# Load order at the start of an S5 plus gated-FFN kernel: the second x tile moves to the common load queue, parameter rows move behind a mean, and the dummy matmuls are cut finer

## The chip, the cores and the metric

The kernel runs on one core of a Trainium2 chip. The metric is the time of one execution in microseconds, as the device measures it. The profile's own span (first to last instruction) is about 1.3 us shorter.

## The reference, cut to what matters

```python
xn = layernorm(x)                                   # x: 2048 x 512, bf16
A  = 2*Re(scan(Lam_bar, xn @ B_bar^T) @ C^T) + xn*Dskip   # Lam_bar = exp(exp(log_dt)*(Lambda_re + i*Lambda_im))
Bo = (gelu(xn @ w_gate) * (xn @ w_up)) @ w_down     # 512 -> 1376 -> 512
out = x + A + Bo
```

The kernel works in 4 blocks of 512 rows, of 4 tiles of 128 rows each. The three parameter vectors (`log_dt`, `Lambda_re`, `Lambda_im`, 1 KB each) are small, but the scan needs them transposed on chip.

## The kernel before

A small list scheduler written in Python orders ScalarE, VectorE and GpSimd statically; TensorE and the load queue (issued by SyncE, "SP") keep the order of the program text. The engines wait for each other by semaphores. In the start, tiles 0 and 1 are only centred (mean taken off), transposed on TensorE and multiplied with the first columns of the weights as these arrive; the division by the root of the variance follows later.

```python
# loads: x tile 0 on the load queue, x tile 1 on ScalarE's queue
ld_x0(0)
GATE["par"] = S.order_behind(ld_x0(1, "scalar", [wrm]), GATE["table"])
for k in range(KD):                       # KD = 4 pieces of 128 KB of each of two weights
    if k in (1, 3):
        ld_x0((k + 3) // 2)               # tiles 2 and 3
    ld_wk(WG, WGc, ins["B_w_gate"], k)
    ld_wk(WU, WUc, ins["B_w_up"], k)
ld_w(WG, WGc, ins["B_w_gate"], 1)
ld_w(WU, WUc, ins["B_w_up"], 1)

def load_par():                           # three rows, on ScalarE's queue, one behind the other
    for q, nm in enumerate(("A_log_dt", "A_Lambda_re", "A_Lambda_im")):
        GATE["par"] = S.order_behind(S.dma(... PROW.ap[4*q:4*q+4, :] ..., queue="scalar", after=[half]), GATE["par"])

def tr_par():                             # on the load queue; waits for all three rows
    S.dma(lambda e: e.dma_start_transpose(PAR.ap..., PROW16.ap), 4096, reads=PROWq, writes=[PAR], tag="tr_par", issue=900.0)
# ... cut ...
nwarm = 7                                 # wide dummy matmuls, so that TensorE's clock rises
PE(fwarm, ...)
def fill(n): ...                          # n narrow dummy matmuls, 128 x 128
# ... cut ...
load_par()
load_W()                                  # the last two weight pieces
tr_par()                                  # <- stands on the load queue AHEAD of all that follows there
S.order_behind(ACT(... X[1] -> NM1 ..., "mean1"), GATE["par"])    # the mean of tile 1, on ScalarE
# ... cut: centring, transposes, first matmuls; then, on the load queue in this order:
#   TR(0): 4 transposes of block 0's x;  ld_x(1): x of block 1;  load_B(): transposed B;  TR(1): block 1's x
```

Of the kernel before, what the change touches and what calls it, by code (L numbers as in the profile page):

```python
# [10 lines left out]
ACTF = mybir.ActivationFunctionType  # L11
# [331 lines left out]
L, D, P, F = 2048, 512, 512, 1376  # L343
# [12 lines left out]
def d_dve_ts4x(n): return 220.0 + 0.26 * n  # L356
D_TINY = 160.0
def d_act(n, ptr=0): return 190.0 + 0.833 * n + 90.0 * ptr
# [3 lines left out]
def build(nc, ins, out):  # L362
    with ExitStack() as es:
        E = es.enter_context
        S = Sched(nc, es)
# [6 lines left out]
        def ring(parent, name, n):  # L372
            return [A.sub(parent, "%s%d" % (name, i), i) for i in range(n)]
# [14 lines left out]
        X = ring(X_all, "X", NT)  # L388
# [73 lines left out]
        ACT = lambda fn, dur, r, w, tag="", after=(): S.op("scalar", fn, dur, r, w, tag, after)  # L462
# [3 lines left out]
        GATE = {"before_gelu": [], "nh": 0}  # L466
        SCR = A.alloc("SCR", [1], F32)
        half = V(lambda e: e.memset(HALF.ap, 0.5), D_TINY, [], [HALF], "half")
        wrm = S.order_behind(V(lambda e: e.memset(WRM.ap, 0.0), 150, [], [WRM], "wrm"), half)
# [5 lines left out]
        NM1, SUM0 = A.alloc("NM1", [1], F32), A.alloc("SUM0", [1], F32)  # L475
# [16 lines left out]
        def ld_x0(j, queue="sync", after=()):  # L492
            return S.dma(lambda e, j=j: e.dma_start(X[j].ap, x2[128 * j:128 * (j + 1), :]), 128 * 1024, writes=[X[j]], tag="ld_x0", queue=queue, after=after)
        ld_x0(0)
        GATE["par"] = S.order_behind(ld_x0(1, "scalar", [wrm]), GATE["table"])
        for k in range(KD):
            if k in (1, 3):
                ld_x0((k + 3) // 2)
# [5 lines left out]
        def load_par():  # L504
            for q, nm in enumerate(("A_log_dt", "A_Lambda_re", "A_Lambda_im")):
                GATE["par"] = S.order_behind(S.dma(lambda e, q=q, nm=nm: e.dma_start(PROW.ap[4 * q:4 * q + 4, :], ins[nm].rearrange("(s p) -> s p", p=128)),
                      1024, writes=[PROWq[q]], tag="ld_" + nm, queue="scalar", after=[half]), GATE["par"])

        def tr_par():
            S.dma(lambda e: e.dma_start_transpose(PAR.ap.rearrange("p q t -> p (q t)").unsqueeze(1), PROW16.ap), 4096,  # L510
                  reads=PROWq, writes=[PAR], tag="tr_par", issue=900.0)
# [12 lines left out]
        def load_W():  # L524
            ld_w(WG, WGc, ins["B_w_gate"], 2)
            ld_w(WU, WUc, ins["B_w_up"], 2)
# [146 lines left out]
        def cent_T(j, k0, k1, bank, eng="A", c0=0):  # L673
            pt = PS[bank].bitcast(BF16)[:, c0:c0 + 128 * (k1 - k0)]

            def f(e):
                ins_ = None
                for k in range(k0, k1):
                    ins_ = e.transpose(pt[:, 128 * (k - k0):128 * (k - k0 + 1)], XN[j].ap[:, 128 * k:128 * (k + 1)], IDN.ap)  # L679
                return ins_  # L680
            PE(f, 56.0 * (k1 - k0), [XNp[j][k0 > 0] if j < 2 else XN[j], IDN], [BANK[bank]], "T0")
            dst, src = XC_all.ap[:, k0:k1, 128 * j:128 * (j + 1)], pt.rearrange("p (q t) -> p q t", t=128)
            w = XCs[j] if k1 - k0 == KD else [XCs[j][k0 > 0]]
            sc = 1.0 if j else 1.0 / D
            if eng == "A":
                GATE["evTA"] = ACT(lambda e: e.activation(dst, src, ACTF.Copy, scale=sc), d_act(128 * (k1 - k0)), [BANK[bank]], w, "evT")
                return GATE["evTA"]
            return V(lambda e: e.tensor_scalar(dst, src, sc, None, ALU.mult), 110 + 0.6 * 128 * (k1 - k0), [BANK[bank]], w, "evT")
# [233 lines left out]
                for j in range(4):  # L922
                    seed(j); hidden(j); states(j); store(j)

        nwarm = 7
        ones, ones4 = nc.const_aps.tensor(1.0, (128, 128), BF16), nc.const_aps.tensor(1.0, (128, 512), BF16)
        wb = 4

# [6 lines left out]
        def fill(n):  # L935
            def f(e):
                ins_ = None
                for _ in range(n):
                    ins_ = e.matmul(PS[wb][:, 0:128], ones, ones, start=True, stop=True)  # L939
                return ins_  # L940
            PE(f, 56.0 * n, [], [BANK[wb]], "fill")
# [3 lines left out]
        def ch(*ops):  # L945
            for op in ops:
                tail_op[0] = S.order_behind(op, tail_op[0])
        def sub(j):
            return V(lambda e: e.tensor_scalar(XN[j].ap, X[j].ap, MVt[0][j].ap[:, 0:1], None, ALU.subtract),
                     d_dve_ts4x(512), [X[j], MVt[0][j]], [XN[j]], "sub")  # L950
        load_par()
        load_W()
        tr_par()
        S.order_behind(ACT(lambda e: e.activation(H0[3].ap[:, 0:D], X[1].ap, ACTF.Copy, scale=-1.0 / D, accum_out=NM1.ap), d_act(512) + 190,
                           [X[1]], [H0[3], NM1], "mean1"), GATE["par"])

        def cent(j, n):
            c0, c1 = (0, 128) if n == 0 else (128, D)
            if j == 0:
                f = lambda e: e.tensor_scalar(XN[j].ap[:, c0:c1], X[j].ap[:, c0:c1], float(D), SUM0.ap, ALU.mult, ALU.subtract)  # L960
            else:
                f = lambda e: e.tensor_scalar(XN[j].ap[:, c0:c1], X[j].ap[:, c0:c1], NM1.ap, None, ALU.add)
            return V(f, 100 + 0.5 * (c1 - c0), [X[j], NM1 if j else SUM0], [XNp[j][n]], "sub")

        ch(V(lambda e: e.tensor_reduce(SUM0.ap, X[0].ap, mybir.AxisListType.X, ALU.add), 600, [X[0]], [SUM0], "sum0"))
        ch(cent(0, 0), cent(0, 1))
        fill(1)
        ch(cent_T(0, 0, 1, 7, "V"))
        ch(cent(1, 0), cent(1, 1))
        fill(4)  # L970
        def ks(k, j, w_, first=False):
            for u in range(2):
                GT_k(k, j, u, w_, first)
# [7 lines left out]
        for j in range(2):  # L981
            ks(1, j, [0, 1])
        ch(*stats(0, 2)); ch(sub(2)); ch(*stats(0, 0)); ch(*stats(0, 1))
        op, mn0, qb0, rq0 = root(0, 0, 3)
        ch(op)
        ch(*stats(0, 3)); ch(sub(3))
        ch(recip(qb0, rq0))
        op, mn3, qb3, rq3 = root(0, 3, 4)
# [63 lines left out]
def bass_parallel_sum__ssm_conv_s5__geglu_ffn__prompt_kernel(  # L1052
    nc: bass.Bass,
    A_x: bass.AP,
    A_Lambda_re: bass.AP,
    A_Lambda_im: bass.AP,
    A_B_re: bass.AP,
    A_B_im: bass.AP,
    A_C_re: bass.AP,
    A_C_im: bass.AP,  # L1060
    A_log_dt: bass.AP,
    A_Dskip: bass.AP,
    B_x: bass.AP,
    B_w_gate: bass.AP,
    B_w_up: bass.AP,
    B_w_down: bass.AP,
    out: bass.AP,
):
    ins = {
        "A_x": A_x, "A_Lambda_re": A_Lambda_re, "A_Lambda_im": A_Lambda_im,  # L1070
        "A_B_re": A_B_re, "A_B_im": A_B_im, "A_C_re": A_C_re, "A_C_im": A_C_im,
        "A_log_dt": A_log_dt, "A_Dskip": A_Dskip,
        "B_w_gate": B_w_gate, "B_w_up": B_w_up, "B_w_down": B_w_down,
    }
    build(nc, ins, out)
# [28 lines left out]
```

## Time and profile before

| | median us | range | runs |
|---|---|---|---|
| before, first series | 177.41 | 177.30 to 177.45 | 6 |
| before, the four later series | 177.41, 177.24, 177.35, 177.31 | 176.95 to 178.19 | 11 each |
| profiled execution of before | 176.98 (span 175.66) | | 1 |

From the page: the span, and the chain that ended last as shares of the span.

```profile
span 175.7 us, 2494 instructions
...
PE 98%; issue 1%; DVE 0%
```

TensorE (PE) is the chain, almost alone. So the time is decided by when TensorE gets going, and by any wait that it meets later. The timeline of TensorE at the start (start us, duration us, engine, line, what, count, and in brackets the idle time before it):

```profile
3.95 0.51 PE L939 MATMUL PS<-const-bfloat16-1.0 128*128 128x128 bf16 x4
4.57 0.38 PE L700 MATMUL PS<-arena 128*128 128x256 bf16 x2
...
7.42 1.02 PE L700 MATMUL PS<-arena 128*128 128x512 bf16 x4
```

L939 are dummies; L700 are the first useful matmuls, at 4.57; the 128x512 ones at 7.42 belong to k=2 and wait for a weight piece that landed at 7.29. Later in the same timeline:

```profile
18.24 5.13 PE L842 MATMUL PS<-arena 128*128 128x512 bf16 x23
23.20 1.48 PE L816 MATMUL PS<-arena 128*128 128x192 bf16 x16
24.52 14.00 PE L748 MATMUL PS<-arena 128*128 128x512 bf16 x70
38.36 1.89 PE L842 MATMUL PS<-arena 128*128 128x512 bf16 x8
```

L842 at 18.24 needs the transposed x of block 0, L748 at 24.52 needs B. No brackets, so no idle time of note.

ScalarE's timeline ("ACTq" is its sequencer, which issues loads):

```profile
0.99 0.38 ACTq L493 DMA_DIRECT2D arena<-in_A_x_dram  x1
1.42 0.57 ACTq L506 DMA_DIRECT2D arena<-in_A_log_dt_dram  x1
2.02 0.26 ACTq L506 DMA_DIRECT2D arena<-in_A_Lambda_re_dram  x1
...
2.31 0.31 ACTq L506 DMA_DIRECT2D arena<-in_A_Lambda_im_dram  x1
...
5.04 1.42 ACT L686 ACTIVATE arena<-PS 128x128 bf16<-128x128 bf16 x3 [1.16 <-PE PS L679]
```

All three rows (L506) have left by 2.6 us, before ScalarE has anything to evict (L686, at 5.04). And the load queue's own timeline:

```profile
8.14 2.37 SPq L510 DMA_TRANSPOSE arena<-arena  x1
10.56 5.18 SPq L735 DMA_TRANSPOSE arena<-arena  x4
15.79 0.58 SPq L478 DMA_DIRECT2D arena<-in_A_x_dram  x1
16.41 3.06 SPq L521 DMA_TRANSPOSE arena<-in_A_B_re_dram  x1
```

L510 is the transpose of the parameters, issued at 8.14, as soon as the last weight piece is off; then the four transposes of block 0 (L735), x of block 1 (L478), B (L521).

### The profile page before, as it was taken

What the parts mean: (1) busy time and instruction counts of PE and PEld (TensorE: products, weight loads), DVE (VectorE), ACT (ScalarE), POOL (GpSimd) and SP (SyncE); (2) the same over time, 40 slices, a digit from 0 to 9 for tenths busy, and PEclk for the clock granted to TensorE, in tenths of its full rate; (3) what the DMA queues carried; (4) which work ended last, traced back from release to release, by engine and by line L of the source; (5) the groups of instructions that cost most, each with busy time, mean ns of one, the idle gap of its engine ahead of it and who ended that gap; (6) DMA issues with size and microseconds to landing.
All of it is one profiled execution on the core that took longest, in us unless ns stands there. A gap on an engine that the chain in (4) does not pass through costs nothing.

```text
span 175.7 us, 2494 instructions
## 1 busy us (share of the span) xinstructions
PE 172.1 (98%) x868; PEld 84.0 (48%) x883; DVE 159.8 (91%) x279; ACT 95.5 (54%) x185; POOL 10.7 (6%) x24
## 2 busy tenths in 40 slices
PE   8999999999999999999999999999999999999995
PEld 3545564644544444444644444444464444444454
DVE  6987999996999989889899999989999899999941
ACT  5476677899876898383576792000667970000000
POOL 3122030201000000002100000000000000000000
DMA  5899999695998000002015000002001000000311
GB/s 155 241 320 174 215 178 222 126 132 113 191 298 225 0 4 2 0 30 85 8 39 111 1 0 0 4 0 90 30 0 30 4 0 0 0 0 0 120 64 60
DMA packets 32420, 14.36 MB, mean 82 GB/s; under 512 B 23736, under 2 KB 32408, under 8 KB 32408
## 3 DMA queue, kind: packets, MB, share of 16 engines
q1 hardware_dynamic: 32240, 14.07, 35.5%
q8 instruction: 7, 0.11, 0.3%
q10 hardware_dynamic: 168, 0.13, 0.2%
q14 instruction: 5, 0.04, 0.1%
HBM read 6.46 MB, written 2.10 MB: 49 GB/s over the span
## 4 chain that ended last, share of the span: by engine, by line
PE 98%; issue 1%; DVE 0%
PE PS L883 37%; PE PS L842 32%; PE PS L748 16%; PE PS L711 4%; PE PS L700 3%; PE PS L816 3%; PE PS L932 2%; PE PS L679 1%; PE PS L939 0%; DVE arena L901 0%
## 5 line engine op out<-in xcount | busy, mean ns | idle before, releaser
L883 PE MATMUL PS<-arena 128*128 128x512 bf16 (+3 forms) x317 | 65.9, 366 | 0.3
L842 PE MATMUL PS<-arena 128*128 128x512 bf16 x257 | 57.1, 379 | 0.4
L883 PEld LDWEIGHTS PS<-arena 128*128 128x128 bf16 (+1 forms) x323 | 30.8, 98 | 35.2
L842 PEld LDWEIGHTS PS<-arena 128*128 128x128 bf16 x264 | 25.8, 98 | 30.2
L786 DVE TENSOR_TENSOR_SCAN arena<-arena 128x512 bf16<-128x512 f32 x32 | 38.9, 1255 | 0.0
L857 ACT ACTIVATE arena<-PS 128x512 bf16<-128x512 f32 x33 | 19.8, 599 | 25.8 <-DVE arena L901 16.7
L748 PE MATMUL PS<-arena 128*128 128x512 bf16 (+1 forms) x134 | 28.0, 366 | 0.1
L861 ACT ACTIVATE arena<-PS 128x512 bf16<-128x512 f32 x33 | 19.8, 600 | 5.1 <-PE PS L842 5.1
L875 ACT ACTIVATE PS<-arena 128x512 f32<-128x512 bf16 (+2 forms) x17 | 9.6, 581 | 19.7 <-DVE arena L901 19.0
L748 PEld LDWEIGHTS PS<-arena 128*128 128x128 bf16 x136 | 13.3, 98 | 14.1
L757 ACT ACTIVATE arena<-PS 128x512 bf16<-128x512 f32 x32 | 17.7, 592 | 2.1 <-PE PS L748 2.1
L901 DVE TENSOR_TENSOR arena<-PS,arena 128x512 bf16<-128x512 f32 (+2 forms) x17 | 10.9, 653 | 6.4 <-PE PS L883 6.4
L863 DVE TENSOR_TENSOR arena<-arena 128x512 bf16<-128x512 bf16 x33 | 13.1, 416 | 1.7 <-ACT arena L861 1.6
L775 DVE TENSOR_TENSOR arena<-arena 128x4096 bf16<-128x4096 bf16 (+1 forms) x5 | 9.2, 1859 | 0.8 <-ACT arena L606 0.8
L773 DVE TENSOR_TENSOR arena<-arena 128x4096 bf16<-128x4096 bf16 (+1 forms) x5 | 9.2, 1859 | 0.1
L798 DVE TENSOR_TENSOR arena<-arena 128x4096 bf16<-128x4096 bf16 x4 | 9.2, 2288 | 0.1
L799 DVE TENSOR_TENSOR arena<-arena 128x4096 bf16<-128x4096 bf16 x4 | 9.1, 2284 | 0.0
L720 ACT ACTIVATE arena<-PS,arena 128x256 bf16<-128x256 f32 (+1 forms) x16 | 6.6, 448 | 3.9 <-PE PS L700 2.1
L610 DVE BATCH_NORM_STATS2 arena<-arena 128x6 f32<-128x512 bf16 x12 | 7.7, 679 | 0.1
L711 PE MATMUL PS<-arena 128*128 128x512 bf16 (+1 forms) x40 | 7.1, 336 | 0.0
L723 DVE SCALAR_TENSOR_TENSOR arena<-PS,arena 128x256 bf16<-128x256 f32 (+1 forms) x16 | 6.3, 445 | 0.5 <-PE PS L700 0.5
L700 PE MATMUL PS<-arena 128*128 128x512 bf16 (+1 forms) x28 | 6.2, 349 | 0.2
(96 smaller groups left out, 124.6 us busy)
## 6 DMA issues: line engine op xcount, KB each, us to landing
out_dram<-arena SPq DMA_DIRECT2D x15, 128.0 KB, 1.7
arena<-in_A_x_dram SPq DMA_DIRECT2D x3, 512.0 KB, 5.3
arena<-in_B_w_down_dram SPq DMA_DIRECT2D x1, 1280.0 KB, 7.2
arena<-in_B_w_gate_dram SPq DMA_DIRECT2D x4, 128.0 KB, 3.0
arena<-in_B_w_up_dram SPq DMA_DIRECT2D x4, 128.0 KB, 3.1
arena<-in_B_w_gate_dram SPq DMA_DIRECT2D x1, 480.0 KB, 6.5
arena<-in_B_w_up_dram SPq DMA_DIRECT2D x1, 480.0 KB, 7.4
arena<-arena SPq DMA_TRANSPOSE x25, 3.1
```

The lines of the kernel that those rows point to most:

```text
L700: PE(lambda e: e.matmul(dst, XCd(j, k), WGU[:, ws[0]:ws[-1] + 1, k, f0:f1], start=first, stop=k == KD - 1, skip_group_check=True), d_pe([w ...
L711: ins_ = e.matmul(dst, XCd(j, k), WGU[:, :, k, f0:f1], start=(k == 0), stop=(k == KD - 1))
L748: ins_ = e.matmul(PS[bank][:, 128 * j0:128 * j1], BBT[c][dk].ap[:, 128 * s:128 * (s + 1)], XNT[b].ap[:, dk, 128 * j0:128 * j1], start=(dk ...
L757: GATE["evBu"] = ACT(lambda e, bank=bank, k3=k3, s=s, c=c: e.activation(SSc[k3][s][c].ap, PS[bank][:, :], ACTF.Copy), d_act(512), [BANK[ba ...
L786: V(lambda e, g=g, rb=rb, init=init: e.tensor_tensor_scan(g.ap, rb, g.ap, init, ALU.mult, ALU.add), d_dve_scan(512), [g, PA[RRr]] + ([CARc ...
L842: ins_ = e.matmul(PS[bank][0:m, c0:c1], W.ap[:, dk, 128 * ft:128 * ft + m], XNT[b].ap[:, dk, c0:c1], start=(dk == 0), stop=(dk == KD - 1))
L857: GATE["last_gelu"] = ACT(lambda e, bg=bg, kk=kk, m=m: e.activation(GG[kk].ap[0:m, :], PS[bg][0:m, :], ACTF.Gelu_apprx_tanh), d_act(512), ...
L861: ACT(lambda e, bu=bu, kk=kk, m=m: e.activation(UPB[kk].ap[0:m, :], PS[bu][0:m, :], ACTF.Copy), d_act(512), [BANK[bu]], [UPB[kk]], "evU")
L863: V(lambda e, kk=kk, m=m, ft=ft, k2=k2: e.tensor_tensor(HTt[k2][ft].ap[0:m, :], GG[kk].ap[0:m, :], UPB[kk].ap[0:m, :], ALU.mult), d_dve_tt ...
L875: ACT(lambda e: e.activation(PS[bank][:, c0:c1], X[tt].ap[:, c0:c1], ACTF.Copy), d_act(c1 - c0), [X[tt]], [BANK[bank]], "seed")
L883: ins_ = e.matmul(PS[bank][:, c0:c1], l_[:, 128 * j:128 * (j + 1)], r_[:, c0:c1], start=False, stop=last and n == len(ops) - 1, skip_group ...
L901: V(lambda e: e.tensor_tensor(OUTB[ko].ap[:, c0:c1], PS[bank][:, c0:c1], XD[tt].ap[:, c0:c1], ALU.add), d_dve_1x(c1 - c0), [BANK[bank], XD ...
```

## The change

The intent, as far as the diff shows it: keep ScalarE's queue clear for the mean of tile 1, keep the tiny row packets out of the way of the first big loads, and close the gaps between dummies with finer ones, so that the clock rises in time.

```diff
         ld_x0(0)
-        GATE["par"] = S.order_behind(ld_x0(1, "scalar", [wrm]), GATE["table"])
+        ld_x0(1)
@@
-        nwarm = 7
+        nwarm = 6
@@
+        GATE["par"] = ACT(lambda e: e.activation(H0[3].ap[:, 0:D], X[1].ap, ACTF.Copy, scale=-1.0 / D, accum_out=NM1.ap), d_act(512) + 190,
+                           [X[1]], [H0[3], NM1], "mean1")
         load_par()
         load_W()
         tr_par()
-        S.order_behind(ACT(... the same ..., "mean1"), GATE["par"])
@@
-        fill(1)
+        fill(3)
         ch(cent_T(0, 0, 1, 7, "V"))
         ch(cent(1, 0), cent(1, 1))
-        fill(4)
+        fill(6)
```

More of the change, by code (lines that the diff above doesn't have):

```diff
@@ L953, in build @@
         tr_par()
-        S.order_behind(ACT(lambda e: e.activation(H0[3].ap[:, 0:D], X[1].ap, ACTF.Copy, scale=-1.0 / D, accum_out=NM1.ap), d_act(512) + 190,
-                           [X[1]], [H0[3], NM1], "mean1"), GATE["par"])
         def cent(j, n):
```

## The prediction

> **What bounds the kernel now.** The page gives TensorE 98% of the chain that ended last. Matmul by matmul, the timeline shows no real stall after 7.42 us: full-width matmuls follow each other every 0.216 us to the end (0.43 us steps that recur every 10 us or so look like missing records). So only what moves the first 7.42 us can move the end, unless the change makes a new stall. In the start, timeline and waits show this chain:
> - x tile 0 issued 0.74, landed 2.82; VectorE sum from 2.84, centering to 3.82, first transpose 3.87, eviction to 4.42, first useful matmul 4.57.
> - small waits for ScalarE evictions (0.15, 0.07, 0.02 us), and at 7.42 a wait for a DMA: the third piece of w_up (k=2) landed 7.29, while TensorE could have gone on at 7.18. That costs 0.25 us and swallows what was won before it.
>
> **What the change does.**
> 1. x of tile 1 moves from ScalarE's queue (issued 0.99, landed 3.13) to second place on the load queue. One issue there takes 0.475 us start to start, so x1 is issued at 1.20 and every weight piece 0.475 us later. The Trainium skill ("Trainium Kernel Development and Optimization", Key Constraints) says that all queues share the same 16 DMA engines and a second issuing engine only saves issue time. The trace agrees: x1's packets run from 2.12 to 2.75, among the tail of x0's. x0 may land 0.05 us earlier, x1 0.1 to 0.3 us later. The mean of tile 1 (0.82 us) then ends about 4.1; it is wanted at 4.34. No loss.
> 2. The third w_up piece is issued at 4.50 instead of 4.02. Its latency was 3.27 us against 2.08 for x0, so it stood in a backlog; the DMA engines are about 90% busy from 2.2 us on. Most of the 0.475 is absorbed. Estimate: it lands between 7.15 and 7.5, so -0.1 to +0.2 us on the end.
> 3. Parameter rows (12 packets of 256 bytes, 15 to 18 ns each) leave after 3.3 instead of 1.42 to 2.3. Too small to matter; their transpose is issued only at 8.1. Their three issues (1.14 us) fall into ScalarE's idle time before 5.04.
> 4. Dummies: one 512-wide matmul less (0.43 us at half clock), four 128-wide more (0.107 each). Before the first transpose they end at 3.60 instead of 3.82. "TensorE: Matmul & The Clock Gate" (The HAM clock gate) puts the rise of the clock after about 3.4 us of activity; here the step of 128-wide matmuls falls from 0.107 to 0.055 us at about 4.2. I expect no change.
> 5. Everything behind on the load queue shifts 0.475 us: the first B transpose landed 23.80, wanted 24.52, so 0.25 us of slack remain.
>
> **Sum.** First useful matmul 0 to 0.1 us earlier, but the wait for w_up of k=2 decides: about zero. Predicted 177.35 us, 8 in 10 between 176.95 and 177.8. Chances: faster by over 2% 0.01, within 2% 0.97, slower 0.02.
>
> **What would show it.** x0 landing near 2.75, first useful matmul near 4.5; x1 landing 3.2 to 3.4, no idle VectorE before the centering of tile 1; matmuls of k=2 starting 7.3 to 7.6 after a wait for w_up; then an unbroken matmul stream of the same length.
>
> **What would make it wrong.** The static scheduler reorders VectorE or ScalarE and opens a stall; parameter issues hold up ScalarE's first eviction; the clock rises a window later; weights land much earlier or later than the backlog suggests; B arrives too late at 24.5.

## More of the kernel before

"Fast" and "slow" are states of an execution. All timed runs that are compared here are marked fast; two runs of e12 and two of e15 are marked slow and are left out of their medians, ranges and ratios.

## The result, and the profile after

| | median us | range | runs |
|---|---|---|---|
| after, first series | 178.69 | 177.93 to 179.19 | 6 |
| before, same series | 177.41 | 177.30 to 177.45 | 6 |

The ratio is 1.0072, 95% interval 1.0049 to 1.0094. Executions over 1.5% slower than the fastest of the same kernel are left out of the means. A ratio here is the mean time of one kernel's fast runs over that of the other's of the same rounds, so it is not quite the ratio of the medians in the table. By the 2% rule this is "the same", but it is a loss clear of noise, and it lies outside the predicted range. The range of the runs is also eight times as wide as that of before in this series; but in the later series single runs of before lay between 176.95 and 178.19, so that part of this contrast is chance.

The chain that ended last in the profiled execution (178.79 us), against the 98% of TensorE shown above:

```profile
span 177.5 us, 2500 instructions
...
PE 85%; DVE 7%; DMA 6%; issue 1%; SPq 1%; DVEq 0%
```

VectorE, DMAs and the load queue now stand in the chain. TensorE at the start:

```profile
4.02 0.85 PE L939 MATMUL PS<-const-bfloat16-1.0 128*128 128x128 bf16 x6
4.66 0.64 PE L700 MATMUL PS<-arena 128*128 128x256 bf16 x2
...
8.02 0.38 PE L700 MATMUL PS<-arena 128*128 128x512 bf16 x1
```

The pair of 128x256 matmuls takes 0.64 instead of 0.38 us: the clock is still low. Matmul by matmul, the step of a 128-wide one falls from 0.107 to 0.055 us at 6.5 us here, at 4.2 before. The matmuls of k=2 start at 8.02, 0.60 us later than before; their weight piece landed at 7.87, in time. Later:

```profile
18.84 5.13 PE L842 MATMUL PS<-arena 128*128 128x512 bf16 x23
23.80 1.48 PE L816 MATMUL PS<-arena 128*128 128x192 bf16 x16
25.44 8.13 PE L748 MATMUL PS<-arena 128*128 128x512 bf16 x39 [0.15 <-DMA arena<-in_A_B_re_dram]
34.11 6.21 PE L748 MATMUL PS<-arena 128*128 128x256 bf16 x31 [0.53 <-DMA arena<-arena]
```

These are the new waits: for B at 25.44, and for the transposed x of block 1 at 34.11. Taking the start of the same matmuls in both profiles gives the account: +0.60 us at 18.84 (minus 18.24), +0.92 at 25.44 (minus 24.52), +1.80 at the first L842 of block 1 (40.16 minus 38.36), and the same +1.80 at the end. So one third came from the start and two thirds, 1.20 us, from waits for late transposes. (The brackets add up to 0.68 us only, since ends of matmuls are modelled. From start to start three steps are longer than before: by 0.32 us at B, and by 0.18 and 0.70 us at two transposes of block 1. The profiled execution of before was a quick one; the medians differ by 1.28 us.)

Where the lateness began, in ScalarE's timeline:

```profile
3.36 0.55 ACTq L506 DMA_DIRECT2D arena<-in_A_log_dt_dram  x1
...
5.44 0.28 ACT L686 ACTIVATE arena<-PS 128x128 bf16<-128x128 bf16 x1 [1.36 <-PE PS L679]
6.18 1.11 ACT L686 ACTIVATE arena<-PS 128x384 bf16<-128x384 bf16 x2 [0.47 <-PE PS L679]
6.82 0.30 ACTq L506 DMA_DIRECT2D arena<-in_A_Lambda_re_dram  x1
7.15 0.31 ACTq L506 DMA_DIRECT2D arena<-in_A_Lambda_im_dram  x1
```

The scheduler left one row behind the mean and put the other two behind the first three evictions (L686). ScalarE takes its instructions in order, so those two rows wait until TensorE has made the transposes that are evicted. The Trainium skill says of the engine queues that ScalarE and VectorE are strict FIFO ("TensorE: Matmul & The Clock Gate", Part 1, Engine queue depths); the trace agrees: the second row leaves at 6.82, when the third eviction has been handed over (6.81). And on the load queue:

```profile
10.65 1.17 SPq L510 DMA_TRANSPOSE arena<-arena  x1
11.87 5.19 SPq L735 DMA_TRANSPOSE arena<-arena  x4
17.10 0.58 SPq L478 DMA_DIRECT2D arena<-in_A_x_dram  x1
17.72 3.30 SPq L521 DMA_TRANSPOSE arena<-in_A_B_re_dram  x1
```

Everything from the parameter transpose on is 1.3 us later or more. The load queue's own waits between 7 and 11 us (what waited, for what: us in total, times, longest) name the row:

```profile
SPq L337 <- DMA arena<-in_A_Lambda_im_dram: 2.1, 1, 2.1
```

Before has no such line. The trace's packet records show why a row of 1 KB takes so long: the last row is issued at 7.15, its last 256-byte packet starts at 10.13, among the packets of the big weight pieces. Issued at 2.31 in the kernel before, it was done with at 3.98.

### The profile page after: what moved, and what is told of

It reads as the page before. It is cut to its first block, busy times and chain, and to the rows that moved or that the text cites. A ratio compares the mean times of both kernels' runs of the same rounds, so it can differ in the third digit from the quotient of the medians.

```text
span 177.5 us, 2500 instructions
## 1 busy us (share of the span) xinstructions
PE 173.2 (98%) x871; PEld 84.6 (48%) x886; DVE 159.9 (90%) x279; ACT 95.4 (54%) x185; POOL 10.6 (6%) x24
## 4 chain that ended last, share of the span: by engine, by line
PE 85%; DVE 7%; DMA 6%; issue 1%; SPq 1%; DVEq 0%
PE PS L883 37%; PE PS L842 29%; PE PS L748 11%; DMA arena<-in_A_x_dram 3%; PE PS L700 3%; PE PS L816 2%; DMA arena<-arena 2%; DVE arena L599 1%; DVE arena L610 1%; DVE arena L723 1%; PE PS L711 1%; DVE arena L629 1%; PE PS L679 1%; SPq L735 1%; DVE arena L964 0%
## 5 line engine op out<-in xcount | busy, mean ns | idle before, releaser
L842 PE MATMUL PS<-arena 128*128 128x512 bf16 x257 | 57.1, 379 | 0.4
L842 PEld LDWEIGHTS PS<-arena 128*128 128x128 bf16 x264 | 25.7, 98 | 30.3
L748 PE MATMUL PS<-arena 128*128 128x512 bf16 (+1 forms) x134 | 28.4, 366 | 0.8 <-DMA arena<-arena 0.5
L711 PE MATMUL PS<-arena 128*128 128x512 bf16 (+1 forms) x40 | 7.1, 336 | 0.0
L700 PE MATMUL PS<-arena 128*128 128x512 bf16 (+1 forms) x28 | 6.9, 381 | 0.0
```

What stands on the lines that cost most here:

```text
L700: PE(lambda e: e.matmul(dst, XCd(j, k), WGU[:, ws[0]:ws[-1] + 1, k, f0:f1], start=first, stop=k == KD - 1, skip_group_check=True), d_pe([w ...
L748: ins_ = e.matmul(PS[bank][:, 128 * j0:128 * j1], BBT[c][dk].ap[:, 128 * s:128 * (s + 1)], XNT[b].ap[:, dk, 128 * j0:128 * j1], start=(dk ...
L842: ins_ = e.matmul(PS[bank][0:m, c0:c1], W.ap[:, dk, 128 * ft:128 * ft + m], XNT[b].ap[:, dk, c0:c1], start=(dk == 0), stop=(dk == KD - 1))
```

## The experiments

Theory L: the loss is the load queue standing still behind two late rows, which makes B and the transposed x late. Its first rivals: C, the finer dummies leave a gap before the first transpose and make the clock rise late; W, the weight pieces come late because x of tile 1 went in front of them. Four series of four kernels were run, each series on one chip together with the kernel before; each kernel has 6 timed runs in its series (e13 has 5), and the profiled execution is one of them, so that its time is known. Two kernels of one series are called mates. All gave correct results. Where an edit says "order list", the static order of one engine was changed after scheduling, so that every other engine's order stays exactly as it was.

### e1_fills_only

Edit, to the kernel before: `nwarm = 6`, `fill(3)`, `fill(6)`, nothing else.

> The kernel before with the new dummies alone (6 wide, then 3, then 6 narrow). Theory L (loads and rows make the loss, dummies harmless): 177.3 to 177.5, matmuls of k=2 start near 7.4 after the wait for w_up. Rival C (the gap that the new dummies leave before the first transpose, 3.60 to 3.94 in the changed kernel, makes the clock rise late): the step of narrow matmuls stays at 0.107 us past 4.6, k=2 starts at 7.7 or later, the time is 177.7 to 178.3 and scatters by over 0.5 us where the kernel before scatters by 0.15.

Measured: 177.19 us (177.10 to 177.76), ratio 0.9991 (0.9971 to 1.0010). The clock rose at 5.2 in the profile, later than 4.2, but k=2 started at 7.60 and no later wait appeared. The dummies alone cost nothing. The late rise spoke for C, and asked for more samples.

### e2_x1_queue_only

```diff
-        GATE["par"] = S.order_behind(ld_x0(1, "scalar", [wrm]), GATE["table"])
+        ld_x0(1); GATE["par"] = GATE["table"]
```

> The kernel before with x of tile 1 second on the load queue, the parameter rows as early as before, old dummies. Theory L: every weight piece issued 0.475 us later lands about that much later; w_up of k=2 lands near 7.8, TensorE waits for it until 7.9 (0.7 us instead of 0.25), time 177.8 to 178.0; no new stall after 10 us. If the backlog absorbs the later issue (as predicted): w_up of k=2 below 7.5 and the time below 177.6. Rival C (clock): clock rises at about 4.2, time 177.4.

Measured: 177.52 us (177.33 to 177.75), ratio 0.9999 (0.9981 to 1.0017). The w_up piece of k=2, issued at 4.50, landed at 7.51: of 0.475 us, 0.22 arrived. Neither expectation hit the landing exactly, but the time says that W costs nothing that can be measured: the new place of x1 is not the loss.

### e3_par_late_only

Edit, to the kernel before, in ScalarE's order list: the mean first, then the first row, three evictions, the two other rows, as in the changed kernel. x of tile 1 stays on ScalarE's queue.

```diff
+        q = S.order["scalar"]     # ... mean1 and rows taken out, then:
+        q[i:i] = [mean, par[0]]   # i: behind the load of x tile 1
+        q[j:j] = par[1:]          # j: behind the third eviction
```

> The kernel before, but on ScalarE's queue the mean of tile 1 comes ahead of the parameter rows and two of the three rows stand behind the first three evictions, just as in the changed kernel; x of tile 1 stays on ScalarE's queue, old dummies, every other engine's order as before. Theory L: the last row lands about 8.5 to 9.5, the transpose of the parameters is issued near 10 instead of 8.14, everything behind it on the load queue is 0.8 us later or so, new stalls of TensorE at 24.5 (B) and near 32 to 34 (transposed x of block 1), together 0.5 to 1.0 us: 177.9 to 178.4. Rival C: 177.4.

Measured: 178.09 us (177.16 to 178.72), ratio 1.0026 (1.0000 to 1.0053). The transpose was issued at 9.84 in the profile. The median moved as expected, but single runs are as quick as the kernel before, and the interval touches 1, so a loss is likely and not clear. The profiled execution is one of the quick ones (177.44) and shows none of the expected stalls at B; the transposes of block 1 cost it 0.19 us.

### e4_after_rows_together

Edit, to the changed kernel, in ScalarE's order list: the three rows directly behind the mean, ahead of the evictions.

```diff
+        q[:] = [o for o in q if o not in par[1:]]
+        i = q.index(par[0]) + 1
+        q[i:i] = par[1:]
```

> The changed kernel with one difference in order: the three parameter rows leave one after the other straight behind the mean of tile 1, ahead of the first eviction. Theory L: transpose of the parameters issued at 8.6 instead of 10.65, the stalls at 25.4 and 32 to 34 us (1.2 us together in the trace) shrink to 0.2 or less, 177.6 to 178.0; what is left is the late start (k=2 near 8.0). If the late stalls come from something else (transposes slower, x1 on the load queue): still 178.4 or more.

Measured: 177.59 us (177.42 to 178.14), ratio 1.0010 (0.9991 to 1.0029). The rows left at 3.42 to 4.31, the transpose was issued at 8.84:

```profile
8.84 1.93 SPq L510 DMA_TRANSPOSE arena<-arena  x1
10.82 5.18 SPq L735 DMA_TRANSPOSE arena<-arena  x4
```

No wait after 11 us is left. So moving two entries of one order list removes the late waits, with x1's new place and the new dummies still in. In time, this is clear against the first series of the changed kernel (1.0072); no unedited changed kernel ran beside e4, and the later series of it (1.0017 to 1.0034) are not clear of e4. Of the change as meant ("rows behind the mean"), this is the version that does only that.

### e5_after_again

The changed kernel, unedited, as a mate of e6 to e8.

> The changed kernel itself once more, as the mate of the three others on one chip. 178.3 to 178.9, parameter transpose issued at 10.5 to 10.8, stalls of TensorE near 25.4 and 32 to 34 us. Theory C (the new dummies make the clock rise late): narrow matmuls change from 0.107 to 0.055 us a piece between 5.0 and 6.6, not at 4.2.

Measured: 177.70 us (177.15 to 178.63), ratio 1.0024 (0.9995 to 1.0053): three runs at 177.15 to 177.41, three at 177.98 to 178.63. The loss of the first series did not return in full. The clock rose early here, with the same new dummies (six of them in 0.51 us):

```profile
3.91 0.51 PE L939 MATMUL PS<-const-bfloat16-1.0 128*128 128x128 bf16 x6
4.49 0.38 PE L700 MATMUL PS<-arena 128*128 128x256 bf16 x2
```

With the clock up, the evictions came early, the last row left at 6.19 and the transpose at 9.06. Expectation C missed: no rise between 5.0 and 6.6. Yet this very execution took 178.24 us, 1.26 over the profiled one of before: TensorE was 0.48 us late at 10 us, after two waits for w_up pieces, and then lost 0.78 us here (0.62 by modelled ends):

```profile
PE PS L842 <- DMA arena<-arena: 0.6, 1, 0.6
```

The fourth transpose of block 0 was issued at 14.94 and landed at 19.15, 4.22 us later; in before it took 2.52 (14.48 to 16.99). So an execution of the changed kernel can be slow although the queue is back on time (first x transpose at 10.65, in before 10.56). Why this landing was late was not found.

### e6_after_old_dummies

Edit, to the changed kernel: `nwarm = 7`, `fill(1)`, `fill(4)`.

> The changed kernel with the old dummies (7 wide, 1 and 4 narrow). Theory C: the clock rises at 4.1 to 4.4 as in the three profiles with old dummies so far, first useful matmul at 4.5 to 4.7; but if the late stalls (B, transposed x) are what bounds the end, the time is no better than the changed kernel's by more than 0.3 us: 178.1 to 178.8. If clock and rows each cost their share and add up: 177.9 to 178.2. If the rise is chance alone: no fixed place of it.

Measured: 177.55 us (177.31 to 178.78), ratio 1.0024 (0.9997 to 1.0051), the same as its mate e5. The profiled execution had a late clock (6.7) with the old dummies. So C as a matter of the dummies falls: in eight profiles each, the rise lay at or before 3.9 to 6.7 us, with the old dummies and with the new ones alike. A small shift of the mean is not excluded. The skill says that the clock's window is free-running and that the point of the rise varies by 0.5 us either way ("TensorE: Matmul & The Clock Gate", Part 1, The HAM clock gate); the chance is there, but these profiles show a spread of 2.8 us.

### e7_transpose_held

Edit, to the kernel before, after scheduling: the parameter transpose also waits for ScalarE's first gelu. The rows leave as early as before.

```diff
+        tr = next(o for o in S.ops if o.tag == "tr_par")
+        tr.deps.append(next(o for o in S.order["scalar"] if o.tag == "gelu"))
```

> The kernel before with every order kept and the rows sent as early as before; only the transpose of the parameters waits, on the load queue, for the first gelu of ScalarE (ends near 10.5), so that it is issued at 10.6 to 10.8 instead of 8.14, as in the changed kernel. Theory L (the loss is the load queue standing still behind the late rows): x of block 1, B and the transposes of block 1 leave 1.2 to 1.4 us later, stalls at about 24.6 and 31 to 34 us, time 178.2 to 178.9. Rival (the late rows themselves, as packets or as time of ScalarE, or the late start do it): 177.3 to 177.6.

Measured: 178.58 us (177.69 to 179.38), ratio 1.0070 (1.0041 to 1.0098), the size of the first series' loss. The queue's timeline has the shape of the changed kernel's:

```profile
10.62 1.18 SPq L510 DMA_TRANSPOSE arena<-arena  x1
11.85 5.18 SPq L735 DMA_TRANSPOSE arena<-arena  x4
```

Its profiled execution is the quickest of the six (177.69), and shows the loss by itself: TensorE was as far at 10 us as in before, and all of the 0.71 us came after that, at late transposes of block 0 and of block 1. With rows, x1, dummies and all orders as before, a load queue that stands still until 10.6 is enough for a loss of this size. The late row packets as traffic, and the time that they take on ScalarE, are not needed for it.

### e8_x2_on_scalar_queue

Edit, to the kernel before: x of tile 2 also goes to ScalarE's queue, the opposite direction of the change.

```diff
-                ld_x0((k + 3) // 2)
+                GATE.update(par=S.order_behind(ld_x0(2, "scalar"), GATE["par"])) if k == 1 else ld_x0(3)
```

> The opposite of the change: the kernel before with x of tile 2 also on ScalarE's queue, behind x of tile 1, so that the weight pieces of k=1 to 3 and all behind are issued 0.475 us earlier. If an earlier issue lands earlier: w_up of k=2 near 6.9 to 7.1, no wait at k=2, 177.0 to 177.2. If the DMA engines are the limit: w_up of k=2 at 7.2 to 7.5 and 177.3 to 177.5 as before. Tile 1's mean may start 0.1 us later because the rows now follow two loads.

Measured: 177.62 us (177.41 to 177.71), ratio 1.0013 (0.9993 to 1.0033). The w_up piece of k=2 did land early (6.77), but the time is no better. In the profile the clock was low until 6.6, so that TensorE came to k=2 only at 8.16. Both expectations missed; where the gain goes when the clock is up was not seen.

### e9_after_rows_early

Edit, to the changed kernel: the rows behind the gelu table and ahead of the mean, as early as before.

> The changed kernel with the parameter rows as early as before (behind the gelu table, ahead of the mean of tile 1); x of tile 1 second on the load queue and new dummies stay. Theory L: parameter transpose issued at 8.6 to 8.7, first transpose of x near 10.7, no stall from B or block 1, 177.3 to 177.7, at or within 0.2 percent of the kernel before, and under its mate e10 by 0.3 to 1.2 us. If the new place of x1 or the dummies cost more than chance: 177.8 or more.

Measured: 177.41 us (177.05 to 177.62), ratio 1.0003 (0.9989 to 1.0016); transpose issued at 8.64, no wait after 7 us. The comparison with the kernel before is as expected. The one with its mate is not: e10 was only 0.07 us slower in the medians.

### e10_after_third

The changed kernel once more.

> The changed kernel, third series, mate of the others. 177.6 to 178.7 with a scatter of 1 us: fast executions near 177.2 where the clock rises by 4.5 and the rows leave near 6, slow ones above 178 where it rises past 6 and they leave near 7. In the profile the last row leaves at 6.1 to 6.3 with an early clock, 7.0 to 7.3 with a late one, and the transpose of the parameters follows 2.8 to 4.4 us later.

Measured: 177.48 us (177.29 to 178.32), ratio 1.0017 (0.9999 to 1.0035): four runs at 177.29 to 177.50, two at 177.96 and 178.32. Last row at 6.65, transpose at 10.19, clock at 5.2, between the two kinds that had been expected.

### e11_held_short

Edit: as e7, but the transpose waits for VectorE's first reciprocal.

> The kernel before, the parameter transpose held on the load queue until the first reciprocal of VectorE (ends 9.3), so issued at 9.4 to 9.7 instead of 8.14. Theory L with a threshold: up to about 9.4 the queue has nothing else to do, because the first transpose of x needs data of 9.8 to 10.1; it starts at 10.6 to 10.9 as before; 177.2 to 177.6, no loss. If any delay of the transpose costs (parameters late for VectorE): 177.9 or more.

Measured: 177.39 us (177.16 to 177.97), ratio 1.0005 (0.9990 to 1.0020). Issued at 9.54, it let the first x transpose go at 10.77; before it was 10.56. So 1.4 us of delay are free: the queue would have waited for VectorE's data anyway. In the trace of before the transpose fills that time with a long issue (2.37 us), here it takes 1.18.

### e12_held_long

Edit: as e7, but it waits for the fifth gelu.

> The kernel before, the parameter transpose held until the fifth gelu of ScalarE (ends near 12.1), so issued at 12.2 to 12.5, 1.6 us later than in e7. Theory L: first transpose of x at 13.4 to 13.7; the transposed x of block 0 lands past 19.5 where TensorE wants it at 18.0, B past 26; loss 1.9 to 3 us, 179.3 to 180.4. If the loss of e7 came from something else than the queue's delay: about 178.5 as e7.

Measured: 181.60 us (179.97 to 182.12) in four runs, ratio 1.0224 (1.0187 to 1.0260); two more, 183.00 and 183.81, are slow. The interval spans the 2% line, so that the verdict is "unclear", though the loss is clear. The direction is right and the size was underestimated: the profiled execution (183.81, slow) waited at L842 for the transposed x of block 0:

```profile
PE PS L842 <- DMA arena<-arena: 3.9, 1, 3.9
```

The fourth transpose of block 0, issued at 18.00, landed at 22.16, so here too the landing took longer than the 2.52 us of before. And the wait is only part of the loss. The trace grants TensorE half the clock from 20.71 to 27.54 us, and the first 24 matmuls of L842 take 7.91 us instead of 5.34: another 2.57 us. Of the 17 other profiles only e15's, the one other with a wait of TensorE of over 1 us, shows such a fall.

### What was open, and e13 to e16

The kind of the loss was clear, its size not: 1.28, 0.46 and 0.13 us in three series. The idea to test was that the clock throws the dice, since the rows wait for evictions, and these for a TensorE at full or half clock.

### e13_warm_before and e14_warm_after

Edit, to the kernel before and to the changed one alike: all loads wait for ten idle `bn_stats` of VectorE (about 6.6 us later), with 32 wide dummies meanwhile and four more behind the landing of x tile 0. The times are meant only for comparison with each other.

> The kernel before with all loads held about 7 us by idle work of VectorE, while wide dummies keep TensorE busy until the first transpose, so that the clock has always risen before the first useful matmul. Only the base for e14: about 7.3 us slower than the kernel before (184.2 to 185.5), and if the chance of the clock makes its scatter, a scatter under 0.4 us. Narrow dummies at 0.055 us a piece throughout.

> The changed kernel with the same hold and the same wide dummies. Theory L with the clock as the dice (a late rise delays the evictions, behind which the rows wait): with the clock always up the rows leave 5.2 to 5.6 us after the issue of x0, as in e5, the parameter transpose follows 8.2 to 9.3 us after it, short of the knee (9.9 us after it), and the median is at most 0.5 us over e13. If landing of the rows (chance in the load traffic), not the clock, decides: rows leave equally early, but the median is still 0.5 us or more over e13 and scatters by 1 us.

Measured: 184.36 us (184.24 to 184.76) and 184.91 us (184.38 to 186.93), so 0.55 us apart; against the kernel before their ratios are 1.0394 and 1.0443. The clock was up in both from 6.2 us on, long before the first useful matmul. The rows left 5.3 and 5.6 us after the issue of x0 and the transpose 8.1 us after it, early as expected, yet one run was 2.6 us over the base's median. By the line drawn beforehand (0.5 us, so passed narrowly), the clock alone does not decide; chance in the landing has a share. The warm profile shows such a case: the transpose of block 0's first tile, issued at 17.12, landed only at 24.08 (issued at 16.98 and landed at 22.38 in e13). Why was not found.

### e15_after_rows_later

Edit, to the changed kernel, in ScalarE's order list: the last two rows behind the fourth eviction instead of the third.

> The changed kernel with one more eviction ahead of the last two rows: they leave at 8.0 to 8.9 instead of 6.2 to 7.2, so their transpose is always past the knee of about 10 us: issued at 11.3 to 12.8. Theory L: 179 to 181, all executions above 178.3. If the delay of the rows is not what counts: as e16.

Measured: 181.21 us (179.99 to 182.10) in the four runs marked fast, ratio 1.0209 (1.0168 to 1.0250), again "unclear" at the 2% line; two more, 182.73 and 183.70, are marked slow. Against its mate e16 (177.95) one more eviction in front of two 1 KB rows cost about 3.3 us. The row is now in the chain that ended last, and the load queue waited for it twice as long as in the changed kernel (the line of the chain, cut by the page itself, then the wait):

```profile
PE PS L883 36%; PE PS L842 33%; PE PS L748 15%; DMA arena<-arena 4%; PE PS L816 3%; DMA arena<-in_A_Lambda_im_dram 3%; PE PS L700 1%; DMA arena<-in_A_x_dram 1%; POOL arena L552 1%; PE PS L679 1%; DVE arena L964 0%; PE PS L939 0%; DVE arena 
```

```profile
SPq L337 <- DMA arena<-in_A_Lambda_im_dram: 4.0, 1, 4.0
```

Here too the clock fell after TensorE's wait (2.8 us at L842), as the page's row of the granted clock, in tenths over 40 slices, shows:

```profile
PEclk9999969999999999999999999999999999999999
```

The first 24 matmuls of L842 took 7.03 us instead of 5.34, so that 1.69 of the 5.12 us that this execution lost belong to the clock. In all six runs each of e12 and e15 the mean clock (1.000, 0.991 or 0.981) falls as the time grows; those at 1.000 (179.97, 179.99 and 180.82) show what the late queue costs without it.

### e16_after_fourth

The changed kernel, mate of e15.

> The changed kernel, fourth series, mate of e15. 177.2 to 178.7, both kinds of executions (near 177.3 and above 178) among six.

Measured: 177.95 us (177.15 to 179.26), ratio 1.0034 (1.0001 to 1.0067): both kinds of executions again.

### The dose, in one table

Each row is one profiled execution. "Late at 10 us" compares the start of the same TensorE transposes at 10 to 11 us with the profile of before; "lost later" is what is added from there to the first L842 of block 1. Their sum is the difference in time of the two executions, to within 0.03 us.

| kernel | why the transpose waits | issued, us | late at 10 us | lost later | this execution, us | ratio to before, all fast runs |
|---|---|---|---|---|---|---|
| before | nothing | 8.14 | 0 | 0 | 176.98 | 1 |
| e9 | nothing (x1 and dummies as changed) | 8.64 | 0.28 | 0 | 177.25 | 1.0003 |
| e4 | rows together behind the mean | 8.84 | 0.74 | 0 | 177.71 | 1.0010 |
| e5 (changed) | two rows behind 3 evictions | 9.06 | 0.48 | 0.78 | 178.24 | 1.0024 |
| e11 | held | 9.54 | 0.20 | 0 | 177.21 | 1.0005 |
| e3 | two rows behind 3 evictions | 9.84 | 0.27 | 0.19 | 177.44 | 1.0026 |
| e10 (changed) | two rows behind 3 evictions | 10.19 | 0.68 | 0.29 | 177.96 | 1.0017 |
| e7 | held | 10.62 | 0 | 0.72 | 177.69 | 1.0070 |
| after, first series | two rows behind 3 evictions | 10.65 | 0.60 | 1.20 | 178.79 | 1.0072 |
| e16 (changed) | two rows behind 3 evictions | 11.35 | 0.67 | 1.59 | 179.26 | 1.0034 |
| e6 | two rows behind 3 evictions | 11.57 | 0.72 | 1.10 | 178.78 | 1.0024 |
| e15 | two rows behind 4 evictions | 12.72 | 0.52 | 4.60 | 182.10 | 1.0209 |
| e12 | held | 12.86 | 0.23 | 6.61 | 183.81 (slow) | 1.0224 |

Up to 9.54 us nothing is lost later, with e5 as the one exception (a late landing that is not explained); from 9.84 on every execution loses, and near 12.8 two quite different ways to be late both lose over 4 us, the fall of the clock included. So, e5 apart, the late queue explains the "lost later" column. The changed kernel lies across that edge: its profiles show 9.06 to 11.35. That fits single executions of it that are as quick as the kernel before (177.15) and others 2 us slower, but e5 shows that it is not the only reason, and runs without a profile can't be assigned. Why all six runs of the first series fell on the slow side stays open.

The "late at 10 us" column does not follow the rows: it is 0.74 in e8 and 0.57 in e2 too, which have early rows. All profiles with x1 on the load queue are later here (0.28 to 0.74) than those with all of x in its old place (0 to 0.27), so W may have a share; the times of e2 and e9 (0.9999 and 1.0003) leave room for at most 0.3 us of it.

No version beat the kernel before clear of noise; e1 was the lowest, its interval includes 1. Of the changed forms, e9 and e4 are level with it.

## Why the prediction was wrong, point by point

- **What bounds the kernel.** Right: TensorE from start to end, and a new stall later was named as the risk; so were a reordering by the scheduler and a late B. All loss of the changed kernel showed as a later start or as waits of TensorE.
- **Step 3, the failing one: "Too small to matter; their transpose is issued only at 8.1. Their three issues (1.14 us) fall into ScalarE's idle time before 5.04."** Only one row left in that time. The diff ties the rows behind the mean but not ahead of the evictions, and the scheduler put three evictions in between; two rows left at 6.82 and 7.15, and took 3 us more among the weight packets. The packets were indeed small; what mattered was who waits for them. With the rows as the prediction had imagined them (e4) the ratio is 1.0010, within the predicted range.
- **Step 5, "everything behind on the load queue shifts 0.475 us".** Mis-sized for the same reason: 1.31 us at the first x transpose (11.87 against 10.56). The slack for B was read rightly (it was wanted at 24.5), and was overrun: a wait for B at 25.44, and a larger one for the transposed x of block 1, which the prediction had not looked at.
- **Step 2, weights.** In the changed kernel's profile w_up of k=2 landed at 7.87, outside 7.15 to 7.5; alone, in e2, at 7.51. In time it cost nothing measurable (ratio 0.9999, at most 0.3 us). The point that issuing from a second queue only saves issue time (the skill, "Trainium Kernel Development and Optimization", Key Constraints) fits: issued 0.475 us later in e2, the piece landed 0.22 us later.
- **Step 4, dummies.** "I expect no change" holds for the time (e1, 0.9991). The reason given was too sure: the clock's rise in the trace of before, 4.2 us, was one throw of a die that shows 3.9 to 6.7.
- **The step that failed, in one sentence:** step 3 assumed the order of the rows on ScalarE (all ahead of 5.04) and did not follow the load queue's wait for them to what stands behind it; instead two rows left at 6.82 and 7.15, the queue waited 2.1 us for the last, and TensorE lost 1.20 us at late transposes.

## What to carry to other kernels

A tiny load is as urgent as the longest queue that waits for it: before moving one, look for who waits on its landing, and what stands behind that waiter in an in-order queue. Tie such a load on both sides (behind this, and ahead of that), or a scheduler will put work that waits for other engines in between. When a change seems to make the runs scatter more, look for an instruction that now waits for something whose time is chance; compare several series before giving the loss a size, and set each profile beside the time of its own execution before an average over others. A wait can cost more than its length: in e12 and e15 the clock fell with it.

## What the Trainium skill lacked or had wrong

- "TensorE: Matmul & The Clock Gate", The HAM clock gate: a spread of the rise of 0.5 us either way is stated; the profiles here show the rise between at most 3.9 and 6.7 us with matmuls from 0.77 us on (the same section does say, further on, that it varies from run to run; and these matmuls have gaps of some 0.3 us among the dummies and first transposes, unlike the back-to-back ones of the page).
- "DMA: Bandwidth & Descriptors", Latency and other measured facts: it gives a floor for tiny transfers (800 ns) and an HBM latency of up to 2 us at high load, not their latency beside a full load queue. Here a row of 4 packets of 256 bytes on the other queue took, from issue to the start of its last packet, 1.67 us in the kernel before (2.31 to 3.98), 2.98 in the changed one (7.15 to 10.13) and 4.22 in e15 (7.98 to 12.20).
- No page that was read warns that a small load put among ScalarE's compute instructions inherits their waits, though the strict order from which it follows is stated: 6.82 instead of about 4.0 for the second row (e4: 4.03), and 1.3 us on the load queue.
